# Attention folded into a mixture-of-experts layer: the first two batches by halves of their tokens, first products begun on 256 columns, and a new order of all steps

## The chip, the cores and the metric

The kernel runs on one core of a Trainium2 chip. The metric is the device time of one execution in microseconds, the median of several runs. The bulk of the work is float32 matrix products on TensorE, each built from three products of high and low parts.

## The reference

```python
def _attn_ref(x, state):                  # x: 8 x 8 x 512 x 64, state: 8 x 8 x 32 x 64
    scale = 1.0 / np.sqrt(D)
    scores = scale * np.matmul(x, state.transpose(0, 1, 3, 2))
    a = softmax(scores)                   # exp(s - max), divided by its sum + 1e-9
    xread = np.matmul(a, state)
    scores2 = scale * np.matmul(state, x.transpose(0, 1, 3, 2))
    a2 = softmax(scores2)
    sread = np.matmul(a2, x)
    return np.concatenate([xread, sread], axis=2)

def _moe_ref(x, w_in, w_out):             # tokens x 512, 512 x 2048, 2048 x 512
    h = np.maximum(x @ w_in, 0.0)
    return h * h @ w_out
```

(The two softmaxes stand in one line each here.) The 8 x 544 rows of the attention's result, with the 8 heads side by side as 512 features, go through the second function; the output is 4352 x 512 float32. The two weights come as float64.

## The kernel before, in words

`tile_attn_moe` treats each batch of 512 tokens as a block (0 to 7) and the 8 x 32 state rows as block 8. It never forms xread: the state of a batch is folded into w_in (`direct_w2`, `second_w2` and later forms make w2 = state times w_in, for 256 of the 2048 columns at a time), and the softmax of a batch, transposed and split into k_hi and k_lo, is multiplied with it. `hidden` (step hidden.BLK.FC) makes one 128-row slice of the 2048 hidden rows for the 512 tokens: six matmuls of 128x512 into a tile ph, then Relu and Square on ACT (or a VectorE form), a cast to g_hi, and on DVE the rest g_lo = ph - g_hi (for some slices PE subtracts instead, with neg_ident). `accumulate` multiplies g_hi and g_lo with wo, w_out decoded and split: eight matmuls of g_hi and four of g_lo for the four acc tiles.

Ahead of this lies the preparation. `load` brings x as tiles xn, `prep` transposes them on PE (px) and copies the result to xT (`evac`, on ACT, or on DVE where the key stands in `SECOND`). `scores` multiplies xT with the states sD into st, `keep_s` copies st to e, `transposed_scores` transposes e (pst), `softmax` takes the maximum m, subtracts (sp), exponentiates on ACT, sums (s), multiplies with the reciprocal (`sm_mul`, on POOL or DVE), transposes back (pa) and writes k_hi on ACT and k_lo on DVE. `exp_s` is the softmax the other way, over the tokens, from the same e. `load_raw`, `decode_wi` and `load_wo`, `prep_wo` bring w_in and w_out as pairs of 32-bit words and decode them: a clamp on DVE or POOL, Prelu on ACT, a shift and a SCALAR_TENSOR_TENSOR on DVE; `decode_wi` also writes the decoded part to memory (win_f), and `prep_wo` splits it with a cast on ACT and a subtraction on DVE or POOL. `warm` issues transposes of ident that nobody reads (pw).

All of this is written as generators with keys, and one table, `PLAN`, lists the keys: each time a key comes up its step goes on to its next `yield`. Everything is held in program order on every engine, so PLAN is the order of the instructions of PE, DVE, ACT, POOL and of the DMA queue of SP; a second table, `SECOND`, chooses sides. The semaphores follow from the data and the buffers. PSUM is given out by three pools: four banks for acc (the first batch's st, px, pst and pa too), two for ph (`ps_h`), two for the rest. Steps have needs (`after`), which only check that PLAN lists them late enough:

```python
            "prep": [key("load", b, 1) if g else key("start", b)],
            "keep_s": [row[key("scores", b)]],
            "exp_s": [key("transposed_scores", b, g)],
...
        ph = ps_h.tile([P, S], F32, tag="ph", name=f"ph{blk}_{fc}")
...
            mm3(ph, pairs)
```

Since all instructions go through one helper, they carry one line in the profile, L429 (L421 in the changed kernel); the names of the tiles tell them apart.

Of the kernel before, what the change touches and what calls it, by code (L numbers as in the profile page):

```python
# [11 lines left out]
F32 = mybir.dt.float32  # L12
# [46 lines left out]
    hidden.1.2 direct_w2.2 direct_w2.2 decode_wi.10 prep_wo.5 hidden.1.1 hidden.1.2 load_wo.7 accumulate.1.0
        hidden.1.1 accumulate.1.1 load_raw.7 decode_wi.6 hidden.1.2  # L60
    hidden.0.4 exp_s.0.0 hidden.1.2 decode_wi.10 decode_wi.7 decode_wi.7 prep_wo.6 hidden.1.2 second_w2.2
        hidden.1.2 prep_wo.4 decode_wi.7 hidden.0.4 prep_wo.5 exp_s.0.0 second_w2.2 load_raw.11 second_w2.2
        second_w2.2 decode_wi.7 transposes.0 load_states.2 decode_wi.7 accumulate.1.1 second_w2.2 prep_wo.8
        decode_wi.11 hidden.0.4 hidden.0.4 hidden.0.4 prep_wo.4 second_w2.2 prep_wo.6
    hidden.1.3 hidden.0.4 decode_wi.11 hidden.1.3 accumulate.1.2 prep_wo.8 load_raw.8 decode_wi.11
        hidden.1.3 hidden.1.3 transposes.0 direct_w2.3 decode_wi.11 decode_wi.8
    hidden.0.5 direct_w2.3 accumulate.1.2 hidden.0.5 decode_wi.8 direct_w2.3 direct_w2.3 hidden.0.5
        hidden.1.3 hidden.1.3 load_raw.9 direct_w2.3 decode_wi.8 hidden.0.5 prep_wo.7 accumulate.1.3
        accumulate.1.3 prep_wo.7 load_wo.13 load_wo.12 direct_w2.3 direct_w2.3 decode_wi.8 second_w2.3
        prep_wo.6 second_w2.3 hidden.0.5 decode_wi.8 accumulate.1.3 transposes.0 accumulate.1.3 decode_wi.9  # L70
        hidden.0.5 accumulate.1.3
    hidden.0.6 second_w2.3 prep_wo.9 accumulate.1.3 hidden.0.6 decode_wi.11 prep_wo.8 load_raw.12
        accumulate.0.4 load_wo.10 decode_wi.9 prep_wo.8 decode_wi.9 second_w2.3 second_w2.3
    hidden.0.7 prep_wo.7 decode_wi.9 hidden.0.6 hidden.0.6 hidden.0.7 hidden.0.7 decode_wi.9 prep_wo.7
        accumulate.0.4 hidden.0.6 hidden.0.7 prep_wo.9 prep_wo.7 prep_wo.8 second_w2.3 hidden.0.7
        accumulate.0.5 hidden.0.6 transposes.0 hidden.0.7 prep_wo.9 load_raw.14 direct.4+direct.5 prep_wo.7
        prep_wo.10 direct_w2.4 direct_w2.5 prep_wo.8 direct_w2.5 direct_w2.4 accumulate.0.5 decode_wi.12
        prep_wo.9 direct_w2.5 direct_w2.4 decode_wi.12
    hidden.1.5
    hidden.1.4 prep_wo.10 states.2 hidden.1.5 prep_wo.12 hidden.1.4 hidden.1.4 accumulate.0.6 direct_w2.4  # L80
        decode_wi.12 hidden.1.4 transposes.0 prep_wo.9 decode_wi.12 decode_wi.14 prep_wo.10 hidden.1.4
        hidden.1.5 prep_wo.10 direct_w2.5 hidden.1.4 accumulate.0.6 load_raw.13 accumulate.0.7 hidden.1.5
        hidden.1.5 decode_wi.14 hidden.1.5 prep_wo.12 exp_s.1.1 prep_wo.9 accumulate.0.7 load_w2.0.4
# [1306 lines left out]
```

## Time and profile before

| | before |
|---|---|
| median of 3 runs | 649.44 us (648.93 to 649.57) |
| profiled execution | 649.0 us, span 647.2 us |
| PE (matmuls) busy | 634.5 us, 98% |
| DVE, ACT, POOL busy | 56%, 54%, 19% |
| chain that ended last | PE 95%, DVE 3%, DMA 1% |
| granted TensorE clock, mean | 0.999 |

One execution was profiled: 647.2 us is its span, 649.0 its time with what lies around it. Busy times are those of instructions; a share of the whole span says little about a stretch with another limit, so the head (up to about 25 us, where the stream of products begins) is read from its own windows and timelines.

### The profile page before, as it was taken

How to read it: one execution, taken by the hardware profiler on the slowest of the kernel's cores; microseconds unless marked ns; L12 is line 12 of the kernel's file. 1: busy time of each engine (PE TensorE's matmuls, PEld its weight loads, DVE VectorE, ACT ScalarE, POOL GpSimd, SP SyncE). 2: the span in 40 equal slices, each digit the busy share in tenths (PEclk: the TensorE clock that was granted, in tenths of full speed). 3: DMA queues.
4: the chain of work that ended last, by engine and by line, in shares of the span. 5: the costliest groups of instructions: out<-in, count | busy, mean ns of one | idle time of the engine just before them, and what ended most of it. 6: DMA issues, size and time to landing. Idle time of an engine off the chain costs nothing.

```text
span 647.2 us, 10790 instructions
## 1 busy us (share of the span) xinstructions
PE 634.5 (98%) x4004; PEld 511.6 (79%) x4004; DVE 365.7 (56%) x658; ACT 348.0 (54%) x678; POOL 125.9 (19%) x96
## 2 busy tenths in 40 slices
PE   5899999999999999999999999999999999999997
PEld 4677777888788878778878878788777888888886
DVE  3999896775756467475347545456354554442322
ACT  3888867656655455365444544455444355444433
POOL 1584343413310220022001310021010101001000
PEclk9999999999999999999999999999999999999999
DMA  8877898988866684463665635352779814240103
GB/s 270 314 233 243 291 283 290 265 266 252 228 179 182 196 253 110 99 169 100 147 163 146 149 82 158 86 124 73 239 239 271 216 46 115 67 145 34 32 1 97
DMA packets 151859, 110.87 MB, mean 171 GB/s; under 512 B 93056, under 2 KB 126080, under 8 KB 151808
## 3 DMA queue, kind: packets, MB, share of 16 engines
q1 hardware_dynamic: 151568, 109.93, 58.7%
q8 instruction: 31, 0.51, 0.3%
q10 hardware_dynamic: 240, 0.26, 0.1%
q14 instruction: 20, 0.16, 0.1%
HBM read 71.89 MB, written 38.27 MB: 170 GB/s over the span
## 4 chain that ended last, share of the span: by engine, by line
PE 95%; DVE 3%; DMA 1%; issue 0%; SPq 0%; ACT 0%; DVEq 0%
PE acc L429 58%; PE ph L429 30%; PE w2ps L429 2%; PE w4ps L429 2%; PE pr L429 1%; PE st L429 1%; DMA xn<-in_x_dram 1%; DVE wf L429 1%; DVE s L429 1%; DVE sp L429 1%; DVE m L429 0%; PE px L429 0%; DVE dec L429 0%; SPq L429 0%; PE pw L429 0%
## 5 line engine op out<-in xcount | busy, mean ns | idle before, releaser
L429 PE MATMUL acc<-wo,g_hi 128*128 128x512 f32 x1090 | 322.4, 391 | 0.0
L429 PEld LDWEIGHTS acc<-wo,g_hi 128*128 128x128 f32 x1090 | 202.8, 188 | 47.4 <-issue 3.4
L429 PE MATMUL acc<-wo,g_lo 128*128 128x512 f32 x545 | 196.7, 389 | 0.0
L429 PE MATMUL ph<-k_hi,w 128*128 128x512 f32 x512 | 172.8, 390 | 0.2 <-DVE w L429 0.2
L429 DVE TENSOR_TENSOR g_lo<-ph,g_hi 128x512 fp32r<-128x512 f32 (+1 forms) x143 | 92.9, 655 | 83.4 <-ACT g_hi L429 81.2
L429 PEld LDWEIGHTS acc<-wo,g_lo 128*128 128x128 f32 x545 | 102.1, 188 | 21.9 <-issue 0.4
L429 ACT ACTIVATE ph<-ph 128x512 f32<-128x512 f32 (+1 forms) x150 | 83.1, 554 | 59.3 <-PE ph L429 49.7
L429 PEld LDWEIGHTS ph<-k_hi,w 128*128 128x128 f32 x512 | 96.0, 188 | 21.4 <-DVE w L429 0.6
L429 PE MATMUL ph<-k_lo,w 128*128 128x512 f32 x256 | 99.8, 390 | 0.0
L429 DVE SCALAR_TENSOR_TENSOR ph<-ph,r 128x512 f32<-128x512 f32 (+1 forms) x69 | 46.7, 676 | 87.8 <-ACT r L429 87.8
L429 ACT ACTIVATE r<-ph 128x512 f32<-128x512 f32 (+1 forms) x69 | 40.3, 583 | 86.6 <-PE ph L429 75.0
L429 POOL TENSOR_TENSOR w<-w_f,w 128x512 fp32r<-128x512 f32 x25 | 32.7, 1309 | 178.5 <-ACT w L429 167.4
L429 PEld LDWEIGHTS ph<-k_lo,w 128*128 128x128 f32 x256 | 48.0, 188 | 10.2 <-DVE k_lo L429 0.3
L429 ACT ACTIVATE g_hi<-r 128x512 fp32r<-128x512 f32 (+1 forms) x69 | 42.4, 616 | 23.1 <-PE acc L429 17.4
L429 ACT CAST g_hi<-ph 128x512 fp32r<-128x512 f32 (+1 forms) x75 | 41.7, 556 | 16.2 <-PE acc L429 14.6
L429 ACT CAST w<-w_f 128x512 fp32r<-128x512 f32 x40 | 24.6, 618 | 17.9 <-DMA w_f<-w_d 14.1
L429 POOL TENSOR_SCALAR dec<-wo_raw 128x512 f32<-128x512 f32 x10 | 20.1, 2012 | 15.3 <-DMA wo_raw<-in_moe_w_out_dram 14.9
L429 POOL TENSOR_TENSOR wo<-dec,wo 128x512 fp32r<-128x512 f32 x12 | 16.7, 1393 | 26.7 <-ACT wo L429 20.4
L429 POOL TENSOR_TENSOR sp<-sp,m 128x512 f32<-128x512 f32 x9 | 9.5, 1052 | 63.8 <-DVE m L429 63.8
L429 POOL TENSOR_TENSOR wf<-wf,wf_hi 128x512 fp32r<-128x512 f32 x8 | 10.5, 1318 | 51.8 <-ACT wf_hi L429 51.7
L429 DVE TENSOR_TENSOR ph<-ph,cross 128x256 f32<-128x256 f32 x16 | 6.9, 432 | 23.7 <-ACT cross L429 23.6
L429 POOL TENSOR_TENSOR s<-sf,s 128x512 fp32r<-128x512 f32 x6 | 7.7, 1292 | 64.8 <-ACT s L429 38.1
(115 smaller groups left out, 597.4 us busy)
## 6 DMA issues: line engine op xcount, KB each, us to landing
w_f<-w_d SPq DMA_DIRECT2D x40, 256.0 KB, 3.4
wi_raw<-in_moe_w_in_dram SPq DMA_DIRECT2D x16, 512.0 KB, 4.8
wo_raw<-in_moe_w_out_dram SPq DMA_DIRECT2D x16, 512.0 KB, 5.9
xr<-in_x_dram SPq DMA_DIRECT2D x16, 512.0 KB, 4.8
wf<-win_f SPq DMA_DIRECT2D x16, 512.0 KB, 4.3
w_d<-w4o SPq DMA_DIRECT2D x32, 256.0 KB, 3.0
w<-w2a_d SPq DMA_DIRECT2D x16, 512.0 KB, 4.5
out_dram<-o SPq DMA_DIRECT2D x31, 256.0 KB, 2.9
```

What stands on the lines that cost most here:

```text
L429: op = call(*args, **kw)
```

## The change

- The tiles xn of the first two batches hold all heads of half of the tokens each, in place of half of the heads and all tokens; `start` loads the first half, `load.B.1` the second.
- Scores of batch 0 are made by halves of the tokens (scores.0.0, scores.0.1), those of both batches with matmuls of 128 columns in place of 256. `keep_s`, `transposed_scores` and `softmax` of batches 0 and 1 go by halves of the tokens too; `keep_s` of batch 0 makes two copies for each half, on the sides that SECOND names.
- Two steps begin.0 and begin.1 (`begin`, `half_hidden`) make the first 256 columns of the products hidden.0.0 and hidden.0.1; `hidden` then does the other half of a tile that was begun.
- PLAN is written anew as a whole, and SECOND with it.

PLAN's place around the first products:

```diff
-        warm.3 load_wo.4 decode_wi.3 prep_wo.0 softmax.0.0 prep_wo.1 decode_wi.3 scores.1 keep_s.1.0
-        keep_s.1.1 softmax.0.1 decode_wi.3
-    hidden.0.0 decode_wi.3 hidden.0.0 hidden.0.0 transposed_scores.1.0 hidden.0.0 load_raw.5 load_wo.6
+        prep_wo.2 prep_wo.0 decode_wi.3 scores.1 softmax.0.1 decode_wi.3 prep_wo.2 begin.1 prep_wo.0
+        softmax.0.1 decode_wi.3 keep_s.1.1
+    hidden.0.1 keep_s.1.0 transposed_scores.1.0 prep_wo.0 transposed_scores.1.1
+    hidden.0.0 decode_wi.3 load_wo.1 decode_wi.3 exp_s.0.0 prep_wo.2 hidden.0.1 softmax.1.1 hidden.0.1
+        softmax.1.0 load_raw.5 begin.0 decode_wi.4 softmax.1.1 hidden.0.1 softmax.1.0 hidden.0.0 hidden.0.0
...
```

SECOND (DVE in place of ACT for keep_s and xT, POOL in place of DVE for the clamps, DVE in place of POOL for sm_mul and w_out_lo), and the code:

```diff
-    decode_wi: 2 4 5 6 14 15
-    decode_wo: 0 3 4 5 6 9 10 12 13 15
+    decode_wi: 4 5 6 8 9
+    decode_wo: 0 3 4 5 6 7 8 9 12 13 14 15
+    keep_s: 0.0.0 0.1.1
-    sm_mul: 0.0 3.0 4.0 4.1 6.1
+    sm_mul: 3.0 6.0 7.1
-    w_out_lo: 3 9 13 15
+    w_out_lo: 0 3 8 11
-    xT: 0.0.0 0.0.1 0.1.1
...
-                xn = p2.tile([P, 4, KC, D], F32, tag="xp", name=f"xn{b}_{g}", bufs=NXP)
+                xn = p2.tile([P, 2 * NC, 2 * D], F32, tag="xp", name=f"xn{b}_{g}", bufs=NXP)
...
-                    nc.sync.dma_start(xn[:, h].rearrange("p h k d -> p h (k d)"), self.rows(g)[:, h])
+                    nc.sync.dma_start(xn[:, ts(c, NC)], self.rows(c)[..., ts(g, 2 * D)])
...
+        def half_scores(self, a):
+            b, calls = self.b, []
...
-                                nc.tensor.matmul, self.st[m][32 * c : 32 * c + 32, o], state_t(b, m, g, c),
-                                self.x[c // 2][64 * m : 64 * m + 64, c % 2, o],
+                                nc.tensor.matmul, self.st[m][32 * c : 32 * c + 32, ts(2 * a + g, P)],
+                                state_t(b, m, g, c), self.x[a][64 * m : 64 * m + 64, c // 2, ts(2 * (c % 2) + g, P)],
...
-        def keep_s(self, g):
+        def keep_s(self, i):
...
+            for m in range(2):
+                if m:
+                    yield
+                evac(f"keep_s.{b}.{i}.{m}", pair[:, i, :, m], st[m][:, i])
...
+    ph_begun = {}
+
+    def half_hidden(fc, ph, a):
+
+        whi, wlo = weights[0, fc // 2]
+        cs, t = ts(fc % 2, P), ts(a, HB)
+        khi, klo = att[0].k
+        pairs = [((whi[:, c, cs], wlo[:, c, cs]), (khi[:, c, t], klo[:, c, t])) for c in range(G)]
+        mm3(ph[:, t], pairs, first=a == 0, skip=True)
+
+    def begin(fc):
+
+        ph_begun[fc] = ps_h.tile([P, S], F32, tag="ph", name=f"ph0_{fc}")
+        half_hidden(fc, ph_begun[fc], 0)
+
     def hidden(blk, fc, nt):
...
-        ph = ps_h.tile([P, S], F32, tag="ph", name=f"ph{blk}_{fc}")
-        if blk == B:
+        ph = None
+        if blk or fc not in ph_begun:
+            ph = ps_h.tile([P, S], F32, tag="ph", name=f"ph{blk}_{fc}")
+        if ph is None:
+            ph = ph_begun.pop(fc)
+            half_hidden(fc, ph, 1)
+        elif blk == B:
...
+    for fc in range(2):
+        step(key("begin", fc), begin, fc, after=[key("softmax", 0, 0), key("direct_w2", 0)])
```

The first place in the order is PE at the first products of block 0 (ph0_0 and ph0_1 are the products 0.0 and 0.1, pst1 transposes of batch 1's e, acc0_0 the first accumulators). In before, from the last part of product 0.0 on:

```order
L429 MATMUL ph0_0_418<-k_hi0_125,w2_0_0_259 128x512
L429 MATMUL pst1_0_430<-ident_73,e21_413 128x128 [waits Activation_49] x2
L429 MATMUL pst1_0_430<-ident_73,e21_413 128x128 x2
L429 MATMUL pst1_1_447<-ident_73,e21_413 128x128 x4
L429 MATMUL ph0_1_459<-k_hi0_125,w2_0_0_259 128x512
L429 MATMUL ph0_1_459<-k_lo0_126,w2_0_0_259 128x512
L429 MATMUL ph0_1_459<-k_hi0_125,w2_0_0_259 128x512 x2
L429 MATMUL ph0_1_459<-k_lo0_126,w2_0_0_259 128x512
L429 MATMUL ph0_1_459<-k_hi0_125,w2_0_0_259 128x512
L429 MATMUL acc0_0_0_471<-wo0_390,g_hi0_0_426 128x512 [waits Activation_49]
```

and in the change, from the last of pst1 on (product 0.1 stands ahead of these rows, in twelve matmuls of 128x256):

```order
L421 MATMUL pst1_1_462<-ident_73,e21_447 128x128 x3
L421 MATMUL ph0_0_467<-k_hi0_125,w2_0_0_267 128x512
L421 MATMUL ph0_0_467<-k_lo0_126,w2_0_0_267 128x512
L421 MATMUL ph0_0_467<-k_hi0_125,w2_0_0_267 128x512 x2
L421 MATMUL ph0_0_467<-k_lo0_126,w2_0_0_267 128x512
L421 MATMUL ph0_0_467<-k_hi0_125,w2_0_0_267 128x512
L421 MATMUL ph0_0_496<-k_hi0_125,w2_0_0_267 128x256 [waits DVE_49]
L421 MATMUL ph0_0_496<-k_lo0_126,w2_0_0_267 128x256
L421 MATMUL ph0_0_496<-k_hi0_125,w2_0_0_267 128x256 x2
L421 MATMUL ph0_0_496<-k_lo0_126,w2_0_0_267 128x256
L421 MATMUL ph0_0_496<-k_hi0_125,w2_0_0_267 128x256
L421 MATMUL ph0_1_436<-g_hi0_1_484,neg_ident_138 128x512 [waits Activation_49]
```

The two products have changed places; product 0.0 is whole, and six matmuls of 256 columns into a second tile ph0_0 follow it, the first with a wait on a DVE semaphore, with neg_ident (for ph0_1) behind them; acc0_0 of g_hi0_0, which followed the products, now comes after neg_ident and w2ps.

The second place is DVE ahead of g_lo0_0 (dec is a part of w_out in decoding, wf of w_in, m11 and sp1 the softmax of batch 1, m20 and nb20 of exp_s.0.0). In before:

```order
L429 TENSOR_SCALAR dec2_440<-wo_raw2_316 128x512 [waits DMAHW4_49]
L429 TENSOR_REDUCE m11_0_444<-pst1_0_430 128x16 [waits PE_49]
L429 TENSOR_REDUCE m11_1_453<-pst1_1_447 128x16 [waits PE_49]
L429 TENSOR_TENSOR sp1_1_452<-pst1_1_447,m11_1_453 128x512 [waits DVE_49,Pool_49]
L429 TENSOR_TENSOR sp1_0_443<-pst1_0_430,m11_0_444 128x512
L429 TENSOR_TENSOR g_lo0_0_427<-ph0_0_418,g_hi0_0_426 128x512 [waits Activation_49]
```

and in the change:

```order
L421 TENSOR_REDUCE m20_0_478<-e20_216 128x1
L421 TENSOR_SCALAR nb20_0_480<-m20_0_478 128x1 [waits DVE_49]
L421 TENSOR_REDUCE m11_1_488<-pst1_1_462 128x16 [waits PE_49]
L421 TENSOR_REDUCE m11_0_492<-pst1_0_456 128x16
L421 TENSOR_TENSOR sp1_1_487<-pst1_1_462,m11_1_488 128x512 [waits DVE_49,Pool_49]
L421 TENSOR_TENSOR sp1_0_491<-pst1_0_456,m11_0_492 128x512 [waits DVE_49,Pool_49]
L421 TENSOR_SCALAR wf2_379<-wf2_379 128x512 [waits DMAHW0_49,Activation_49]
L421 TENSOR_SCALAR dec1_513<-wo_raw1_475 128x512 [waits DMAHW6_49]
L421 SCALAR_TENSOR_TENSOR wf2_379<-wi_raw4_363,wf2_379 128x512 [waits DMAHW3_49,DVE_49]
L421 TENSOR_TENSOR g_lo0_0_508<-ph0_0_467,g_hi0_0_507 128x512 [waits Activation_49]
```

g_lo0_0 was the 38th instruction of DVE and is the 42nd; the reduction and nb of exp_s.0.0 and a part of wf2 now stand just ahead of it.

The third place is the DMA queue of SP at its start (xn0_0 and xn0_1 are the x of batch 0, two DMAs each). In before:

```order
L429 DMA xn0_0_127<-in_x_dram 128x2x256 x2
L429 DMA wi_raw0_130<-in_moe_w_in_dram 128x2x512
L429 DMA std0_134<-in_state_dram 128x2x64
L429 DMA xn0_1_136<-in_x_dram 128x2x256
L429 DMA wi_raw1_145<-in_moe_w_in_dram 128x2x512
L429 DMA xn0_1_136<-in_x_dram 128x2x256
L429 DMA std0_134<-in_state_dram 128x2x64
L429 DMA std0_134<-in_state_dram 128x2x64 [waits DMAHW0_49]
L429 DMA wo_raw1_169<-in_moe_w_out_dram 128x1024 [waits DMAHW1_49]
L429 DMA win_f0_77<-wf0_132 128x512 [waits DMAHW2_49,DVE_49]
```

and in the change:

```order
L421 DMA xn0_0_127<-in_x_dram 128x4x128 x2
L421 DMA wi_raw0_133<-in_moe_w_in_dram 128x2x512
L421 DMA std0_149<-in_state_dram 128x2x64 x3
L421 DMA wi_raw1_161<-in_moe_w_in_dram 128x2x512
L421 DMA xn0_1_172<-in_x_dram 128x4x128
L421 DMA win_f0_77<-wf0_140 128x512 [waits DMAHW0_49,DVE_49]
L421 DMA xn0_1_172<-in_x_dram 128x4x128 [waits DMAHW1_49]
L421 DMA wi_raw2_205<-in_moe_w_in_dram 128x2x512 [waits DMAHW2_49]
```

The second DMA of xn0_1 stood ahead of win_f0, and now stands behind it; win_f0 waits on a DVE semaphore.

## Rows read from the trace of the kernel before

**Rows 1.** The page, part 1: busy us (share of the span) xinstructions of each engine.

```profile
PE 634.5 (98%) x4004; PEld 511.6 (79%) x4004; DVE 365.7 (56%) x658; ACT 348.0 (54%) x678; POOL 125.9 (19%) x96
```

**Rows 2.** Waits of PE over the whole span: us in total, times, longest.

```profile
PE ph L429 <- DVE w L429: 0.2, 1, 0.2
```

**Rows 3.** Windows: busy us of PE, PEld, DVE, ACT, POOL (instructions), PEclk, DMA share, GB/s.

```profile
8.10:11.20 3.10, 3.05 (x15) 3.02 (x16) 2.78 (x6) 1.61 (x4) 0.00 (x0) 1.00 1.01 349
20.00:31.30 11.30, 10.01 (x91) 7.51 (x98) 11.09 (x21) 9.83 (x20) 6.10 (x5) 1.00 0.83 287
```

**Rows 4.** Timeline of PE, 24 to 36 us: start us, us, engine, instruction, count [idle before].

```profile
24.27 1.09 PE L429 MATMUL st<-xT,sD 64*32 64x256 f32 x32
25.30 0.51 PE L429 MATMUL ph<-k_hi,w 128*128 128x512 f32 x1
...
29.14 2.02 PE L429 MATMUL acc<-wo,g_hi 128*128 128x512 f32 x8
...
32.45 1.09 PE L429 MATMUL acc<-wo,g_lo 128*128 128x512 f32 x4
...
34.85 0.73 PE L429 MATMUL ph<-k_hi,w 128*128 128x512 f32 x2 [0.18 <-DVE w L429]
```

**Rows 5.** Timeline of DVE from 18 to 33 us.

```profile
21.54 1.28 DVE L429 TENSOR_SCALAR wf<-wf 128x512 uint32<-128x512 uint32 x1
...
30.56 0.68 DVE L429 TENSOR_TENSOR g_lo<-ph,g_hi 128x512 fp32r<-128x512 f32 x1
```

**Rows 6.** Timeline of ACT from 25 to 33 us.

```profile
25.70 1.06 ACT L429 COPY e<-st 128x512 f32<-128x512 f32 x2
27.08 1.20 ACT L429 ACTIVATE ph<-ph 128x512 f32<-128x512 f32 x2 [0.32 <-PE ph L429]
28.31 0.59 ACT L429 CAST g_hi<-ph 128x512 fp32r<-128x512 f32 x1
```

**Rows 7.** Groups of DVE, 7 to 31.3 us: busy us, mean ns of one | idle before.

```profile
L429 DVE TENSOR_SCALAR wf<-wf 128x512 uint32<-128x512 uint32 x4 | 3.0, 761 | 0.8 <-ACT wf L429 0.7
...
L429 DVE TENSOR_REDUCE m<-pst 128x16 f32<-128x512 f32 x4 | 2.7, 685 | 1.1 <-PE pst L429 1.1
L429 DVE COPY xT<-px 128x512 f32<-128x512 f32 x3 | 2.1, 686 | 0.5 <-PE px L429 0.5
...
L429 DVE TENSOR_SCALAR wf<-wi_raw 128x512 f32<-128x512 f32 x3 | 1.3, 426 | 7.2 <-DMA wi_raw<-in_moe_w_in_dram 7.2
...
L429 DVE TENSOR_TENSOR sp<-sp,s 128x512 f32<-128x512 f32 x1 | 0.7, 677 | 0.0
```

**Rows 8.** Groups of DVE, 14 to 60 us.

```profile
L429 DVE TENSOR_TENSOR w<-w2ps,w 128x256 fp32r<-128x256 f32 x7 | 2.9, 408 | 0.1
```

**Rows 9.** Timeline of POOL from 17 to 32 us.

```profile
21.26 1.27 POOL L429 TENSOR_TENSOR wo<-dec,wo 128x512 fp32r<-128x512 f32 x1
```

**Rows 10.** Timeline of PE from 636 to 641 us (six rows of 128x256 from first to last).

```profile
637.07 0.40 PE L429 MATMUL acc<-wo,g_hi 128*128 128x256 f32 x2
...
637.79 0.63 PE L429 MATMUL acc<-wo,g_hi 128*128 128x512 f32 x2
```

**Rows 11.** Timeline of SP (its DMA issues) from 0 to 26 us.

```profile
3.78 0.47 SPq L429 DMA_DIRECT2D xn<-in_x_dram  x1
...
9.98 0.34 SPq L429 DMA_DIRECT2D win_f<-wf  x1
...
13.94 0.74 SPq L429 DMA_DIRECT2D xn<-in_x_dram  x1
```

**Rows 12.** DMA issues, 0 to 40 us: KB each, median us to landing.

```profile
xn<-in_x_dram SPq DMA_DIRECT2D x8, 256.0 KB, 5.9
```

**Rows 13.** Timeline of PE from 7 to 13 us.

```profile
8.15 1.97 PE L429 MATMUL px<-ident,xn 128*128 128x128 f32 x8 [2.09 <-DMA xn<-in_x_dram]
...
11.19 0.68 PE L429 MATMUL px<-ident,xn 128*128 128x128 f32 x4
```

**Rows 14.** Tile pw: duration ns min/median/max, first and last start us.

```profile
L429 PE MATMUL pw<-ident x24: 270/372/421, 4.6 to 24.1; 128*128 128x128 f32 x24
```

More of the change, by code (lines that the diff above doesn't have):

```diff
@@ L59 @@
[L59 to L83, printed above, removed]
-        accumulate.0.7 accumulate.0.7 prep_wo.10 prep_wo.12
-    hidden.1.6 load_w2.0.4 accumulate.0.7 prep_wo.10 decode_wi.12 accumulate.0.7
@@ new lines @@
+    hidden.4.11 last_w2.2 transposes.4 load_w2.5.0 hidden.4.10 hidden.4.11 hidden.4.10 hidden.4.11
+        hidden.4.11 start.7 softmax.5.1 hidden.4.11 exp_s.5.1 hidden.4.11 softmax.5.0
+    hidden.4.12 accumulate.2.15 load_w2.4.7 hidden.4.12 accumulate.4.9
+    hidden.4.13 softmax.5.0 hidden.4.13 accumulate.4.10 hidden.4.12 hidden.4.13 softmax.5.0 load_w2.5.0
+        hidden.4.12 load_w2.5.1 exp_s.5.0 softmax.5.1 softmax.5.1 hidden.4.12 hidden.4.13 hidden.4.12
+        accumulate.4.11 transposes.4
@@ new lines @@
+    hidden.6.6 softmax.7.0
+    hidden.6.8 accumulate.6.4 hidden.6.8 hidden.6.8 hidden.6.6 last_w2.6 hidden.6.6 accumulate.6.5
+        softmax.7.0 hidden.6.8 hidden.6.8 hidden.6.6 hidden.6.8 hidden.6.6 softmax.7.1
+    hidden.6.7 last_w2.6 hidden.6.7 load_wi.0 hidden.6.7 hidden.6.6 w2.7+read.6 hidden.6.7 accumulate.6.6
+        softmax.7.0 exp_s.7.0 transposes.7 load_wi.0 sread.6 hidden.6.7 last_w2.7 hidden.6.7 last_w2.7
+        transposes.7
+    hidden.6.9 sread.6 sread.6 hidden.6.9 hidden.6.9 hidden.6.9
@@ L363 @@
 """
 ROWS = """
-    scores.0
     scores.1
@@ L646, in prep @@
                 pt = pool.tile([P, S], F32, tag=tag, name=f"px{b}_{g}_{c}")
[L647 to L650 removed]
+                for i in range(NC):
+                    nc.tensor.transpose(pt[:, ts(i, P)], self.xn[g][:, NC * c + i], ident)
                 yield
@@ L1267, in needed, with scores_0 @@
         }[kind]
+    def scores_0(a):
+        if a == 0:
+            att[0].st = {m: ps_acc.tile([P, S], F32, tag="acc", name=f"st0_{m}") for m in range(2)}
+        in_a_row(att[0].half_scores(a))
     row = {}
+    for a in range(2):
+        step(key("scores", 0, a), scores_0, a, after=[key("prep", 0, a), [key("states", 0), key("scores", 0, 0)][a]])
+    row["scores.0"] = key("scores", 0, 1)
     for members in [line.split() for line in ROWS.strip().split("\n")]:
@@ L1296, in tile_attn_moe @@
                 del after["keep_s"]
+            else:
+                after["exp_s"] = [key("transposed_scores", b, i) for i in range(G)]
+            if b == 0:
+                after["keep_s"] = [key("scores", 0, g)]
+                after["transposed_scores"] = [key("keep_s", 0, g)]
             for name, needs in after.items():
```

666 lines of the change are left out of this document (333 added, 333 removed), and 3 rows, old and new, of the table SECOND.

## The prediction

> **What bounds the kernel.** I read the page first: TensorE (PE) is busy for 634.5 us, 98% of the span, VectorE (DVE) for 365.7, 56% [rows 1]. The waits of PE come next: the only wait of a product for an operand is one of 0.2 us [rows 2]. So PE is the bound. Time can be won in the head, before the stream of products begins at 25.30 us, or lost where something new stops that stream. The windows then tell who sets the pace of the head: from 20.0 to 31.3 us DVE works 11.09 of 11.30 us [rows 3]. While PE enters its stream, DVE has no slack at all; the whole argument rests on this. The timeline of PE gives the places: scores of batch 1 at 24.27, first product at 25.30, the first acc at 29.14, with the transposes pst and the second product between these two [rows 4].
>
> **What the new order does.** The diff means to begin the first two products early, on 256 columns. In the order of PE that is not what stands there. begin.1 comes after scores.1 and the last pa, and is followed at once by the other half of the same product: twelve matmuls of 256 columns where six of 512 stood. And hidden.0.0 stands ahead of begin.0, so product 0.0 runs whole, and begin.0 then fills a second tile ph0_0 with six matmuls of 256 columns that nobody reads. That tile takes the PSUM bank of the first one, so its first matmul waits on DVE for the bank's last reader, the subtraction g_lo0_0. PE works in order: behind that wait stand neg_ident, the 32 w2ps of block 1, all of acc 0.0 and product 0.2, and none of these needs g_lo0_0 or its bank, but for the last four of acc. In before PE waited for nothing there: behind the product stood pst, the second product and acc, and g_lo0_0 was wanted only at 32.45, by the last four matmuls of acc [rows 4].
>
> **The wait, step by step.** In before g_lo0_0 ran from 30.56 to 31.24 [rows 5], while its product was done when Relu began, at 27.08 [rows 6]: 4.2 us. Its own chain is shorter: Relu and Square 1.20, cast 0.59 [rows 6], subtraction 0.68 [rows 5], some 2.5 us. The other 1.7 us is the queue of DVE. So DVE's queue sets the time at which the new wait ends, and I count that queue. In before 37 instructions stand ahead of g_lo0_0 on DVE, now 41. Gone are three copies of xT (3 x 0.686) and one multiply of sp (0.677) [rows 7], 2.74 us; they go to ACT and POOL. New are one clamp of wf (0.43), one shift (0.43 where nothing blocks it, like the clamp), one SCALAR_TENSOR_TENSOR and one reduction m<-e (like the other reduction, 0.69 each), one subtraction for wo (like the multiply, 0.68) [rows 7], nb (128x1, at most a clamp; I take 0.2), and two copies of half an e, 256 columns each (like the 128x256 w, 0.41 [rows 8]): 3.9 us. That is net +1.1 us in a stretch without slack. I add 0.3, because the multiply that left DVE now runs on POOL, and a shift of wf beside a POOL instruction took 1.28 us, 0.85 more than a clamp [rows 5, 7, 9]. So g_lo0_0 ends at about 31.24 + 1.4 = 32.65.
>
> [...]
>
> PE does the same useful work up to there: product, pst and second product took from 25.30 to 29.14, 3.84 us [rows 4]. The pieces of 256 columns cost little: six start within 0.72 us (637.07 to 637.79 [rows 10]), twelve 1.44, where the six of 512 were part of the 3.84 with about 1.4. With the start unchanged PE reaches begin.0 at 29.2 and stands until 32.65: a **wait of about 3.4 us** in one piece. Then come the six unread matmuls, 0.72 us.
>
> **The start.** This is the term I know least, and it cancels: as long as DVE sets the end of the wait, an earlier start only makes the wait longer. The first half of x (two DMAs ahead of all) can go on alone, but the second DMA of the other half now stands on SP behind win_f, which waits for the first decoded w_in: it was issued at 3.78 us, win_f at 9.98 [rows 11], and an x takes 5.9 us more to land [rows 12]. The copies of xT are all on ACT now, and both pa and the scores of batch 1 stand ahead of the first product on PE. Bounds: not before batch 1's x is there (13.94 + 5.9 = 19.8 [rows 11, 12]), transposed (four in 0.68 [rows 13]), copied (like e, 0.53 [rows 6]) and scored (1.09 [rows 4]), 22.1; not much after the 1.4 us that DVE is later, 26.9 with a little queueing. I take 25.3, the old start, since DVE is as full before it as it was.
>
> **The sum.** What began at 29.14 in before (acc and w2ps) begins when g_lo0_0 is done and the unread matmuls are through: 32.65 + 0.72 - 29.14 = +4.2 us. PE's wait of 0.18 at 34.85 was for w of DVE [rows 4]; behind the long wait DVE has caught up, so I take off 0.2. The rest of the program keeps its matmuls, and before's PE waited for nothing in it [rows 2]. The new sides of decode, squares and stores there I cost at nothing, because PE's stream covers them: DVE is busy for 56% of the span [rows 1], so a us put on it there moves nothing; without that cover each would cost its own 0.4 to 0.7 us. Sum +4.0: the profiled execution, 649.0, becomes 653.0. The median of the runs, 649.44, lies 0.4 above that execution, and I forecast **653.3**.
>
> Bounds of that sum: at the low end DVE uses up all it stood idle in this stretch (1.1 + 0.5 + 0.7 [rows 7]) and the 0.85 of the long shift, g_lo0_0 ends at 31.24 + 1.1 - 3.15 = 29.2, and the total is +0.6, 649.6 to 650.0; its own chain behind the earliest start would end at 22.1 + 3.9 + 2.5 = 28.5, so DVE decides there too. At the high end it ends 2 us later (two more long shifts, or a late wo_raw, whose clamp stands just ahead of it): 655.3.
>
> **The rivals.** About 0.2%, 1.3 us, is what a measurement of this kernel can tell from no change.
>
> Slower pace after the wait (0.20). In the trace eight transposes at 8.15 us took 1.97 us, and four at 11.19 only 0.68 [rows 13]. [...] If a wait of 3.4 us brings that back, 3.0 us at half pace cost 1.5 us: 654.8. For it: the wait is longer than the 2.09 us of idle time ahead of 8.15. Against it: the trace has no stop in mid-stream that shows it.
> [...]
>
> DVE later by 1.5 us (0.08): 654.8 as well, by blocked shifts or by the DMA of wo_raw.
>
> DVE early (0.10): with the copies gone DVE runs ahead, g_lo0_0 ends at 29.2 to 29.6, PE waits for it hardly at all: 649.6 to 650.4, no change that can be told.
>
> Faster (0.08): begin.0 doesn't do what its place in the order says, its product is dropped or finds its bank free, and PE does not stop. Then each us by which the first product starts before 25.3 is won, at most 3.2 (22.1); half of that gives 647.8. It decides at a start of about 24.0. For it: the first half of x needs only the two DMAs ahead of all. Against it: 24 unread transposes pw run in the trace of before [rows 14], and the wait stands in the order.
>
> **The numbers.** Forecast 0.54 (652 to 654.5), pace 0.20, DVE later 0.08, DVE early 0.10, faster 0.08. The range leaves out "faster", most of "DVE early" and a little above: 650.2 to 656.2. Faster by over 0.2%: 0.08; within: 0.09, nearly all of "DVE early"; slower: 0.83.
>
> **What would show it.** In the waits of PE one entry of 3 to 4 us of ph for DVE's g_lo; in the groups, eighteen matmuls 128x256 of ph<-k at the head; in the timeline g_lo0_0 ending at 32 to 33 and the first product at 25; behind the wait matmuls at twice their old spacing if the pace falls, at the old one if not. I am wrong if that entry is missing or under 1 us, or if PE waits for more than 1 us in all after 40 us.

## The result, and the profile after

The changed kernel takes 656.34 us (median of 4 runs, 655.82 to 657.57), the kernel before 649.51 (648.93 to 650.01) beside it: a ratio of 1.0104 [1.0090, 1.0117], 6.8 us slower. The forecast was 653.3 with a range from 650.2 to 656.2. The profiled execution took 657.57 us, 1.2 above its median, so local times below are larger than what the medians tell.

The page of the changed kernel, part 1 and the group of the products' matmuls in part 5:

```profile
PE 641.4 (98%) x4080; PEld 515.4 (79%) x4080; DVE 358.7 (55%) x659; ACT 345.6 (53%) x675; POOL 132.0 (20%) x100
...
L421 PE MATMUL ph<-k_hi,w 128*128 128x512 f32 (+1 forms) x520 | 175.9, 390 | 3.6 <-DVE g_lo L421 3.2
```

PE is busy 6.9 us longer than in [rows 1], with DVE 7.0 us less: DVE's total says nothing of the loss. The group's idle time has a new releaser, g_lo. Waits of PE in the changed kernel (us in total, times, longest):

```profile
PE ph L421 <- DVE g_lo L421: 3.2, 1, 3.2
...
PE pr L421 <- DMA xr<-in_x_dram: 0.5, 1, 0.5
PE ph L421 <- DVE w L421: 0.3, 1, 0.3
```

One entry of 3.2 us stands where [rows 2] had 0.2; the other two lie behind 40 us. Its place, in the timeline of PE (start us, us, engine, instruction, count [idle before]), from the scores of batch 1 on:

```profile
24.94 1.45 PE L421 MATMUL st<-xT,sD 64*32 64x128 f32 x64
26.32 0.39 PE L421 MATMUL ph<-k_hi,w 128*128 128x256 f32 x1
...
27.85 1.04 PE L421 MATMUL pst<-ident,e 128*128 128x128 f32 x8
...
29.88 0.40 PE L421 MATMUL ph<-k_hi,w 128*128 128x512 f32 x1
33.49 0.58 PE L421 MATMUL ph<-k_hi,w 128*128 128x256 f32 x1 [3.21 <-DVE g_lo L421]
...
34.93 0.63 PE L421 MATMUL ph<-g_hi,neg_ident 128*128 128x512 f32 x1
35.49 1.96 PE L421 MATMUL w2ps<-wf,sD 64*32 64x256 f32 x32
37.38 2.98 PE L421 MATMUL acc<-wo,g_hi 128*128 128x512 f32 x8
40.20 0.39 PE L421 MATMUL ph<-k_hi,w 128*128 128x512 f32 x1
...
651.57 0.39 PE L421 MATMUL acc<-wo,g_lo 128*128 128x512 f32 x1
```

The first product starts at 26.32 (25.30 in [rows 4]). PE stands before the unread product, and everything behind it is slow: the six matmuls take 1.44 us (33.49 to 34.93) where six took 0.72 [rows 10], eight acc 2.98 where [rows 4] have 2.02. The windows of the same kernel (busy us of PE, PEld, DVE, ACT and POOL, then PEclk, DMA share, GB/s) say why:

```profile
28.00:32.00 4.00, 2.28 (x15) 1.67 (x12) 3.97 (x9) 3.90 (x8) 3.44 (x3) 1.00 0.58 187
32.00:33.00 1.00, 0.00 (x0) 0.00 (x0) 1.00 (x3) 0.76 (x2) 0.00 (x0) 0.72 0.43 164
33.00:35.00 2.00, 1.51 (x7) 1.51 (x7) 1.09 (x2) 0.00 (x0) 1.83 (x1) 0.50 0.64 198
35.00:39.00 4.00, 4.00 (x38) 2.05 (x38) 1.04 (x3) 1.44 (x4) 0.12 (x1) 0.50 0.95 341
39.00:40.00 1.00, 1.00 (x6) 0.77 (x5) 0.97 (x2) 1.00 (x3) 0.00 (x0) 0.86 0.99 406
40.00:42.00 2.00, 2.00 (x10) 1.65 (x9) 1.89 (x6) 0.75 (x3) 1.67 (x2) 1.00 0.25 102
```

The granted clock falls from 1.00 to 0.50 while PE stands, and comes back only in the slice from 39 to 40. Last, DVE and ACT around g_lo0_0:

```profile
32.15 0.68 DVE L421 SCALAR_TENSOR_TENSOR wf<-wi_raw,wf 128x512 uint32<-128x512 uint32 x1
32.75 0.68 DVE L421 TENSOR_TENSOR g_lo<-ph,g_hi 128x512 fp32r<-128x512 f32 x1
```
```profile
30.31 1.20 ACT L421 ACTIVATE ph<-ph 128x512 f32<-128x512 f32 x2
31.54 0.59 ACT L421 CAST g_hi<-ph 128x512 fp32r<-128x512 f32 x1
```

g_hi is there at 32.13, g_lo0_0 runs from 32.75 to 33.43.

The last matmul of the program started at 643.03 in the profile of before and starts at 651.57 now. These 8.5 us are accounted for by:

| place | us | from |
|---|---|---|
| later first product | +1.0 | 26.32 - 25.30 |
| PE stands for g_lo0_0 | +3.4 | 33.49 - (29.88 + 0.23) |
| unread product at the full clock | +0.7 | six starts, [rows 10] |
| half clock from the unread product to acc | +2.7 | (40.20 - 33.49) - 0.72 - (32.45 - 29.14 of [rows 4]) |
| small gaps of before up to 35 us that are gone | -0.4 | the remainder up to 42 us |
| behind 42 us | +1.1 | small gaps; 0.5 and 0.3 of them stand in the waits above |

### The profile page after: what moved, and what is told of

Read it like the earlier page. It is cut to its first block, busy times and chain, and to the rows that moved or that the text cites. A ratio compares the mean times of both kernels' runs of the same rounds, so it can differ in the third digit from the quotient of the medians.

```text
span 655.8 us, 10979 instructions
## 1 busy us (share of the span) xinstructions
PE 641.4 (98%) x4080; PEld 515.4 (79%) x4080; DVE 358.7 (55%) x659; ACT 345.6 (53%) x675; POOL 132.0 (20%) x100
## 4 chain that ended last, share of the span: by engine, by line
PE 87%; DMA 5%; DVE 3%; ACT 2%; issue 1%; SPq 1%; POOL 0%; DVEq 0%; ACTq 0%
PE acc L421 52%; PE ph L421 28%; PE w2ps L421 3%; DMA wi_raw<-in_moe_w_in_dram 2%; PE w4ps L421 2%; PE pr L421 1%; DMA xp<-in_x_dram 1%; PE st L421 1%; DVE wf L421 1%; SPq L421 1%; DMA xr<-in_x_dram 1%; DMA e_d<-turned 1%; DMA w_d<-w2o 0%; ACT xT L421 0%; DVE w4o L421 0%
## 5 line engine op out<-in xcount | busy, mean ns | idle before, releaser
L421 PE MATMUL ph<-k_hi,w 128*128 128x512 f32 (+1 forms) x520 | 175.9, 390 | 3.6 <-DVE g_lo L421 3.2
L421 ACT ACTIVATE ph<-ph 128x512 f32<-128x512 f32 (+1 forms) x164 | 92.3, 565 | 82.2 <-PE ph L421 78.2
L421 PE MATMUL ph<-k_lo,w 128*128 128x512 f32 (+1 forms) x260 | 101.0, 388 | 0.0
L421 DVE SCALAR_TENSOR_TENSOR ph<-ph,r 128x512 f32<-128x512 f32 (+1 forms) x62 | 41.1, 662 | 78.4 <-ACT r L421 78.3
L421 ACT ACTIVATE r<-ph 128x512 f32<-128x512 f32 (+1 forms) x62 | 35.2, 571 | 86.2 <-PE ph L421 79.9
L421 ACT CAST g_hi<-ph 128x512 fp32r<-128x512 f32 (+1 forms) x82 | 46.5, 567 | 18.0 <-PE acc L421 16.2
L421 ACT ACTIVATE g_hi<-r 128x512 fp32r<-128x512 f32 (+1 forms) x62 | 37.4, 604 | 18.7 <-PE acc L421 13.3
L421 POOL TENSOR_TENSOR s<-sf,s 128x512 fp32r<-128x512 f32 x9 | 11.9, 1326 | 111.4 <-ACT s L421 71.4
L421 POOL TENSOR_TENSOR sp<-sp,s 128x512 f32<-128x512 f32 x13 | 14.0, 1078 | 40.4 <-DVE s L421 26.1
L421 DVE COPY w4o<-w4ps 128x512 f32<-128x512 f32 x21 | 13.8, 683 | 11.7 <-PE w4ps L421 8.8
```

What stands on the lines that cost most here:

```text
L421: op = call(*args, **kw)
```

## The experiments

Three theories stood against each other: that the stop for g_lo0_0 alone costs what is lost (the forecast); that the pace behind the stop costs as much again (the rival with 0.20); and that the rest of the new order loses time even without the stop. Ratios are to the kernel before on the same chip, whose medians lay between 649.30 and 649.77.

### The stop taken away in two ways: e1_begin_first and e2_no_begin0

```diff
-    hidden.0.0 decode_wi.3 load_wo.1 ...
-        softmax.1.0 load_raw.5 begin.0 decode_wi.4 ...
+    begin.0 hidden.0.0 decode_wi.3 load_wo.1 ...
+        softmax.1.0 load_raw.5 decode_wi.4 ...
```

> The changed kernel with begin.0 ahead of hidden.0.0, so that its six matmuls are the first half of product 0.0 and nothing is computed in vain. Theory A (the misplaced begin.0 costs its wait of 3.4 us, its 0.7 us of unread matmuls and about 2.9 us of matmuls at the lower clock behind the wait): 656.3 - 7.0 = 649.4, no wait of ph for g_lo, granted clock 1.00 from 30 to 40 us. Rival B (the wait only shows that DVE is late; without it PE waits for the same DVE a little later, at the first acc and at product 0.2): short waits of 1.5 to 2.5 us in sum, clock 1.00, about 651.5.

```diff
-        softmax.1.0 load_raw.5 begin.0 decode_wi.4 ...
+        softmax.1.0 load_raw.5 decode_wi.4 ...
-    for fc in range(2):
+    for fc in range(1, 2):
```

> The changed kernel without begin.0 at all: product 0.0 in six matmuls of 512 columns. Theory A: 649.3; rival B: 651.4. Against the run with begin.0 ahead of the product it tells what the cut into 256 columns costs for this product: 0.06 us by its spacing, nothing that can be measured; if the cut itself were worth anything, this run would be slower by over 0.5.

Measured: 652.60 [1.0031, 1.0061] and 652.62 [1.0030, 1.0058]. In both the stop is gone and the clock reads 1.00 from 25 to 45 us. Half of the loss goes with begin.0's place: 3.7 us in the medians. The other half stays: 3.1 us, with no wait of PE over 0.9 us behind the first product in either. What stays shows in the trace of e2_again, the same kernel run once more (below): its only wait of PE between 26 and 46 us, and the weight loads (PEld) at 31 us:

```profile
PE pa L421 <- DVE w L421: 0.7, 1, 0.7
```
```profile
31.19 0.19 PEld L421 LDWEIGHTS ph<-g_hi,neg_ident 128*128 128x128 f32 x1 [0.53 <-ACT g_hi L421]
...
32.28 0.61 PEld L421 LDWEIGHTS w2ps<-wf,sD 64*32 64x32 f32 x30 [0.40 <-DVE sp L421]
```

and in its windows (columns as above):

```profile
30.00:35.00 5.00, 4.82 (x45) 2.79 (x44) 5.00 (x11) 4.94 (x11) 3.81 (x3) 1.00 0.58 188
35.00:40.00 5.00, 5.00 (x23) 4.12 (x23) 4.86 (x10) 4.58 (x11) 3.21 (x4) 1.00 0.98 326
40.00:45.00 5.00, 4.28 (x23) 3.46 (x23) 4.96 (x10) 3.83 (x10) 5.00 (x4) 1.00 0.40 157
```

The same 15 us in the kernel before:

```profile
30.00:45.00 15.00, 14.78 (x94) 10.96 (x94) 14.01 (x28) 12.12 (x26) 12.89 (x9) 1.00 0.77 276
```

DVE works 14.8 of 15 us in e2_again, but 14.0 in before too, where PE hardly waits; so a full DVE alone does not explain it. In e2_again PE waits for DVE at 42 us, and at 31 us loads weights late, behind ACT and DVE: neg_ident and w2ps take from 30.93 (last product at 30.70, 0.23 each) to acc at 33.30, 2.4 us, where the same two take 0.32 + 1.02 behind the fill of e6 (next section). Together that is 1.7 us. The profiled executions split what stays. In six without a stop (e1, e2's two, and e5, e9 and e10 below; e12 has a longer wait of its own) the first product starts 0.9 to 2.2 us later than in [rows 4] (26.17 in e9, 27.45 in e2), and from it to the last matmul it takes 1.5 to 2.9 us longer (619.2 in e2, 620.6 in e1, against 643.03 - 25.30 = 617.7).

The start differs as much between executions. Seven of the profiled executions have the new order unchanged up to the first product (the changed kernel, e1, e2, e2_again, e3, e11, e12); it starts between 25.50 (e11) and 27.79 (e3). In before and two variants with its head (e4, e8) it starts between 25.08 and 25.39. The three latest of the seven are e2's two and e3, and in these the clock of the head read lower, as in this window of e2_again, where the changed kernel, e1 (from 21 us on) and e12 read 1.00 and e11 has four px in 0.60 us at 22.12 (1.06 at 23.08 in e2):

```profile
20.00:25.00 5.00, 4.21 (x25) 4.15 (x26) 3.83 (x9) 4.28 (x10) 2.07 (x2) 0.66 1.07 386
```

### The stop filled, so that the clock holds: e3_fill, e6_fill_head and e7_after_head

```diff
     def begin(fc):
...
+        if fc == 0:
+            fill = ps_acc.tile([P, S], F32, tag="acc", name="fill")
+            for _ in range(14):
+                nc.tensor.matmul(fill, weights[0, 0][0][:, 0, :P], att[0].k[0][:, 0], start=True, stop=True)
```

> The changed kernel with 14 unread matmuls of 128x512 into a free bank between product 0.0 and begin.0, some 3.2 us of work at 0.227 us each, so that TensorE works where it stood; the wait for g_lo0_0 ends when it did. If the clock falls because TensorE stands still: granted clock 1.00 from 30 to 40 us, and the 2.9 us are back, 656.3 - 2.9 = 653.4. If the fall of the clock had another cause, or the slow matmuls behind the wait were slow for lack of operands: 656.3 as before, with the clock at 0.5 in the same place.

Measured 655.86 [1.0080, 1.0115], a miss: only 0.5 us less than the changed kernel. The clock did hold (1.00 from 28 to 42 us), and from pst to the product ph_2 it took 9.60 us instead of 12.35. But in this execution's head the clock read 0.50 between 11 and 14 us and 0.66 between 20 and 25, and the first product came at 27.79. So the head was given 24 more unread transposes, with the fill and without it:

```diff
-    WARM = 12
+    WARM = 24
-        ... load.0.1 states.0 scores.0.0
+        ... load.0.1 states.0 warm.12 warm.13 warm.14 warm.15 warm.16 scores.0.0
-        ... second_w2.0 warm.2 prep.1.0
+        ... second_w2.0 warm.2 warm.17 warm.18 warm.19 warm.20 warm.21 warm.22 warm.23 prep.1.0
```

> The changed kernel with the head filled in the same way and, besides, the 14 unread matmuls in the wait for g_lo0_0. If the half clock behind the wait is worth what the first profile shows (2.75 us from pst to product 0.2: 12.35 against 9.60), this run is faster than the one with the filled head alone by 2.5 to 3: about 652.8. If a fall of the clock costs nothing in the end: the same as that one.

> The changed kernel with the head filled, and the wait for g_lo0_0 left empty: the control for the run before it. 656.3 less what a falling clock in the head costs in some executions, 655.5; mean clock 0.995, from the wait alone.

e6 took 653.65 [1.0037, 1.0081], e7 655.60 [1.0071, 1.0114]: 1.95 us, though the intervals overlap. The timelines of PE show the mechanism where it acts. With the fill, then with PE left standing:

```profile
33.17 0.38 PE L423 MATMUL ph<-k_hi,w 128*128 128x256 f32 x1
...
34.31 1.09 PE L423 MATMUL w2ps<-wf,sD 64*32 64x256 f32 x32
35.33 2.12 PE L423 MATMUL acc<-wo,g_hi 128*128 128x512 f32 x8
37.29 0.40 PE L423 MATMUL ph<-k_hi,w 128*128 128x512 f32 x1
```
```profile
33.03 0.39 PE L423 MATMUL ph<-k_hi,w 128*128 128x256 f32 x1 [3.06 <-DVE g_lo L423]
...
34.17 1.71 PE L423 MATMUL w2ps<-wf,sD 64*32 64x256 f32 x32
35.81 3.08 PE L423 MATMUL acc<-wo,g_hi 128*128 128x512 f32 x8
38.73 0.39 PE L423 MATMUL ph<-k_hi,w 128*128 128x512 f32 x1
```

The same instructions take 4.12 us with the fill and 5.70 without, 1.6 more; in the changed kernel 6.71, 2.6 more. The granted clock of e7 in the stretch behind its stop:

```profile
33.00:35.00 2.00, 1.97 (x31) 1.50 (x39) 0.39 (x1) 0.00 (x0) 1.42 (x1) 0.88 0.93 234
35.00:38.00 3.00, 3.00 (x23) 1.80 (x6) 1.66 (x4) 2.06 (x6) 0.00 (x0) 0.51 0.97 343
```

In e6 it reads 1.00 in both. So the pace behind the stop is the clock, and costs 1.6 to 2.7 us on PE's path. That this comes out at the end of the kernel is borne by the two medians alone: e6's profiled execution takes 655.72, e7's 654.63, and from first product to last matmul 623.6 against 622.6, since in e6's PE waits again at 88 and 92 us, 0.3 us for wo of POOL and 1.6 us for g_lo.

The falls behind g_lo0_0's wait came behind idle time of PE, 3.21 us in the changed kernel and 3.06 in e7, and none came where the fill took its place (1.00 in e3 and e6); but in e7 it came after PE had resumed (last section).

With its stop filled, begin.0 costs nothing that the medians show: e6 and the kernel without begin.0 and with the same head (e5, next) both take 653.65. Their intervals reach 1.3 to 1.4 us to either side, and in the profiled executions the way from first product to last matmul is 3.2 us longer in e6 (623.6 against 620.4); so this equality is not firm.

### The head: e5_no_begin0_head, e9_x_ahead, e10_x_ahead_dve

e5 is e2 with the head's 24 transposes as above.

> The changed kernel without begin.0, and with 24 unread transposes more in the head: 10 ahead of the first scores (where TensorE stood for sD) and 14 ahead of batch 1's first px (where it stood for x), some 1.1 and 1.5 us of work. Theory: the new head leaves TensorE so little to do at 8 to 10 and 19 to 21 us that the clock falls in some executions; with the holes filled it reads 1.00 in all, and the median falls from 652.62 to 651.5 (the two executions without begin.0 whose mean clock was 1.000 took 651.47 and 651.71). Rival: the clock of the head costs nothing that counts, since DVE sets the start of the products: 652.6, or more by what the transposes delay.

Measured 653.65 [1.0039, 1.0078], with the clock at 1.000 in four of five executions. The median did not fall, but the filling has a price of its own: in the chain that ended last, 18 unread transposes, 14 of them the new ones, stand ahead of batch 1's px (start us, us, what), and the first product comes at 27.25 (at 26.15 and 26.01 in e6 and e7, whose head is the same):

```profile
19.71 2.20 PE pw L423 x18
```

So e5 does not tell the head's clock from its own transposes; e9 does. It is e2 with the second half of x issued ahead of win_f:

```diff
-        prep.0.0 load.0.1 prep.0.0 states.0 warm.11 decode_wi.0 decode_wi.1 load.0.1 states.0 scores.0.0
+        prep.0.0 load.0.1 load.0.1 prep.0.0 states.0 warm.11 decode_wi.0 decode_wi.1 states.0 scores.0.0
```

> The changed kernel without begin.0, and with the second DMA of batch 0's other half of x ahead of win_f on SP, as in the kernel before (issued at about 4.9 in place of 10.4 us). If this DMA is what makes the head late (the products of the four profiles of the new head start 1 to 2.5 us behind before's 25.30): px of that half at 11 to 12 us in place of 13, and the products up to 1.5 us earlier, 651.2. If DVE or ACT sets the start anyway: px earlier, the products not, 652.6 as without begin.0.

and e10 gives DVE its three copies of xT back on top of that:

```diff
+    xT: 0.0.0 0.0.1 0.1.1
```

> The same with three of batch 0's copies of xT back on DVE, 2.1 us of it, as in the kernel before. If ACT is what is late in the new head: 0.5 to 1 us earlier than the run before it. If DVE is: up to 2 us later.

Measured 652.65 [1.0029, 1.0059] and 652.62 [1.0033, 1.0060], with first products at 26.17 and 26.29. Neither the order of x nor the side of xT holds the 3.1 us. Nor does the head's clock: the four executions of e9 with a mean clock of 1.000 took 651.50 to 653.01, 2.2 to 3.7 us more than before. It may hold a part, since e2's two executions at 1.000 took 651.47 and 651.71 and its other three 652.62 to 653.59.

### A stop in the kernel before: e4_before_dead

```diff
+    def dead(n):
...
+        ph = ps_h.tile([P, S], F32, tag="ph", name="dead")
...
+        mm3(ph[:, :HB], pairs, skip=True)
-    hidden.0.1 softmax.1.0 hidden.0.1 ...
+    hidden.0.1 dead.0 softmax.1.0 hidden.0.1 ...
```

> The kernel before with the misplaced product alone: six unread matmuls of 256 columns into a new ph tile behind the second product. They wait for g_lo0_0, which ends at 31.24, from 29.14 on: 2.1 us of wait and 0.7 us of matmuls. If the clock holds through a wait of 2.1 us: 649.5 + 2.8 = 652.3, less a few tenths. If it falls here too, for as long as in the changed kernel: 655.

Measured 652.44 [1.0029, 1.0059], a hit. Timeline of PE and a window of this kernel:

```profile
31.38 0.39 PE L429 MATMUL dead<-k_hi,w 128*128 128x256 f32 x1 [1.98 <-DVE g_lo L429]
...
32.20 2.00 PE L429 MATMUL acc<-wo,g_hi 128*128 128x512 f32 x8
```
```profile
30.00:35.00 5.00, 3.62 (x46) 2.63 (x46) 3.04 (x7) 1.72 (x4) 4.51 (x4) 1.00 1.02 383
```

An unread product that waits for g_lo0_0 costs wait and matmuls, 1.98 + 0.82, and here the clock reads 1.00 behind it: eight acc take their 2.00 us. The price of such a stop is its length plus, in some stops (1.6 us behind 3.06 in e7), the clock.

### The product's own chain, or DVE's queue: e11_glo_early

```diff
-        hidden.0.0 hidden.0.0 decode_wi.4 prep_wo.1 decode_wi.4 prep_wo.1 ...
-        load_raw.6 hidden.0.0 accumulate.0.0 ...
+        hidden.0.0 hidden.0.0 hidden.0.0 decode_wi.4 prep_wo.1 decode_wi.4 prep_wo.1 ...
+        load_raw.6 accumulate.0.0 ...
```

> The changed kernel, begin.0 and all, with g_lo0_0 three instructions earlier on DVE (ahead of the two of wf2 and the clamp of dec1, 1.5 us). If DVE's queue sets the end of the wait, as the prediction had it: the wait 1.5 us shorter, 654.8 or less. If the product's own chain does (in the changed kernel's trace g_hi0_0 is cast until 32.13, and g_lo0_0 began at 32.75): 0.6 us shorter, 655.7.

Measured 655.60 [1.0074, 1.0111], a hit for the chain. With three instructions fewer ahead of it, g_lo0_0 stands idle for ACT's g_hi (timeline of DVE):

```profile
31.34 0.69 DVE L421 TENSOR_TENSOR g_lo<-ph,g_hi 128x512 fp32r<-128x512 f32 x1 [0.47 <-ACT g_hi L421]
```

PE still waits 2.6 us. DVE's queue held the end of the wait for 0.6 us only (32.13 to 32.75 in the changed kernel); the rest is Relu, Square and cast on ACT and the subtraction. The clock falls behind this shorter stop too (window as above, PE resumed at 32.09):

```profile
33.00:35.00 2.00, 2.00 (x35) 0.87 (x33) 1.10 (x2) 0.37 (x1) 1.56 (x1) 0.50 0.21 73
```

### The later order alone: e8_late_order

The order and sides of before up to its hidden.0.4, the new order and sides from its hidden.0.4 on:

```diff
-    hidden.0.4 exp_s.0.0 hidden.1.2 decode_wi.10 decode_wi.7 decode_wi.7 prep_wo.6 ...
+    exp_s.0.0 second_w2.2 exp_s.0.0 second_w2.2 ...
+    hidden.0.4 accumulate.1.1 decode_wi.8 transposes.0 ...
```

> The kernel before up to product 0.4 (about 62 us) in code, order and sides, and from there the changed kernel's order and sides. The changed kernel's profile shows four waits of TensorE behind 60 us that before's has not (at 78, 93, 144 and 526 us), 1.3 us in all. If they belong to the late order itself: 650.8. If they come from the late head: 649.5, as before.

Measured 655.68 [1.0073, 1.0112]: a miss, since the seam between the two orders makes a stop of its own. Timeline of PE and the window behind it:

```profile
58.23 1.10 PE L89 MATMUL w2ps<-wf,sD 64*32 64x256 f32 x32 [2.78 <-DVE wf L89]
...
59.93 1.05 PE L89 MATMUL ph<-k_hi,w 128*128 128x512 f32 x2
60.78 0.63 PE L89 MATMUL ph<-k_lo,w 128*128 128x512 f32 x1
```
```profile
58.50:63.00 4.50, 4.50 (x42) 3.23 (x27) 2.88 (x6) 2.30 (x6) 2.68 (x2) 0.64 0.47 138
```

The clock falls here too, behind 2.78 us. Of the 5.4 us by which the stretch from first product to last matmul grew (623.11 against 617.73), 2.8 is the stop and some 1.5 the clock (3.3 us of matmuls 0.43 apart instead of 0.23); about 1 us would be left for the later order. With the seam's own work in it, that stays a bound.

### DVE relieved: e12_less_dve and the control e2_again

e2 with wo0's subtraction back on POOL, and the reduction and nb of exp_s.0.0 behind the product 0.2: some 1.5 us less on DVE up to there.

```diff
-    hidden.0.0 decode_wi.3 load_wo.1 decode_wi.3 exp_s.0.0 prep_wo.2 ...
+    hidden.0.0 decode_wi.3 load_wo.1 decode_wi.3 prep_wo.2 ...
-        hidden.0.2 decode_wi.5 exp_s.0.1
+        hidden.0.2 decode_wi.5 exp_s.0.0 exp_s.0.1
-    w_out_lo: 0 3 8 11
+    w_out_lo: 3 8 11
```

> The changed kernel without begin.0, and with two of DVE's new pieces put elsewhere: wo0's subtraction back on POOL, and the reduction and nb of exp_s.0.0 behind product 0.2 in the order; 1.5 us less of DVE ahead of g_lo0_0. Without begin.0 DVE is busy for 14.2 of 15 us from 30 to 45 us while TensorE stands for 0.2 and 0.8 us. If DVE's queue is what is left of the loss of 3.1 us: 651.2 to 651.5. If it is the head ahead of 25 us, or POOL (5.00 of 5 us at 40 to 45) takes DVE's place: 652.6 or later.

> The control on the same chip: the changed kernel without begin.0 once more, 652.6.

Measured 655.39 [1.0066, 1.0093] against 653.05 [1.0032, 1.0059] for the control: this way of taking work from DVE made it 2.3 us slower. DVE and POOL in e12:

```profile
32.31 1.50 DVE L421 TENSOR_SCALAR dec<-wo_raw 128x512 f32<-128x512 f32 x1
33.73 1.14 DVE L421 SCALAR_TENSOR_TENSOR wf<-wi_raw,wf 128x512 uint32<-128x512 uint32 x1
34.79 0.68 DVE L421 TENSOR_TENSOR g_lo<-ph,g_hi 128x512 fp32r<-128x512 f32 x1
...
42.04 0.67 DVE L421 TENSOR_REDUCE m<-e 128x1 f32<-128x512 f32 x1
...
43.60 0.41 DVE L421 TENSOR_TENSOR w<-w2ps,w 128x256 fp32r<-128x256 f32 x1
```
```profile
32.08 1.45 POOL L421 TENSOR_TENSOR wo<-dec,wo 128x512 fp32r<-128x512 f32 x1
33.49 2.14 POOL L421 TENSOR_SCALAR wf<-wi_raw 128x512 f32<-128x512 f32 x1
```

The clamp takes 1.50 us beside POOL's subtraction (0.42 in the changed kernel), the SCALAR_TENSOR_TENSOR 1.14 (0.68 above), and g_lo ends at 35.47 (34.10 in the control). PE's wait for w behind it grows from 0.7 to 1.9 us. This w comes 2.1 us later than in the control (43.60 against 41.50): 1.4 us of it is there when g_lo ends, and the rest is about what the moved reduction and its nb take (0.8 us from 42.04 on), which now stand ahead of this w with those of exp_s.0.1. So e12 took work away from one wait and put part of it ahead of the next, and does not tell what a relieved DVE would be worth.

The clamp ends at 33.81, 0.3 us behind POOL's subtraction (33.53). The SCALAR_TENSOR_TENSOR ends at 34.87, while POOL's instruction beside it runs to 35.63. What held the two up is not shown.

## Why the prediction was right in kind and too low in size

The step that failed is the sum behind the stop: it left out the pace, and put the start ("it cancels") and the rest of the program ("I cost at nothing") at nothing. Along PE's path in the profiled execution the runs show in its place a half clock that cost 2.7 us, a start 1.0 us later and 1.1 us of gaps behind 42 us. By taking begin.0 away they show that 3.7 us go with it and 3.1 us stay. The two accounts differ because the stop covers waits that come to light once it is gone.

- **The mechanism held, the wait's length in part by luck.** begin.0's product is made whole and read by nobody, its first matmul waits for g_lo0_0, and the wait stands as one entry: 3.2 us idle, 3.4 with the last product's 0.2, as forecast. But both of its ends came later than forecast by about the same: PE reached begin.0 at 30.1, not 29.2, and g_lo0_0 ended at 33.43, not 32.65. The groups show twelve k_hi and six k_lo matmuls 128x256, the eighteen foreseen. Faster or unchanged did not come.
- **The pace was mis-sized, and given too little chance.** "Against it: the trace has no stop in mid-stream that shows it" was true of the trace of before, and I set 0.20 on it and 1.5 us. Its 3.0 us were the way from 8.15 to 11.19 in [rows 13], its half pace my estimate, which no row of before shows; the runs showed 0.50 for some 6.8 us in the changed kernel, and 0.50 to 0.51 for some 3.3 us in e7 and e11. It came: clock 0.50, at a cost of 1.6 us (e7 against e6, local), 1.95 (their medians) or 2.7 (the profiled execution). Along PE's path it is the largest term that the sum lacks: the profiled execution lies 4.5 us above the sum, of which the pace is 2.7, the later start 1.0 and the gaps behind 42 us 1.1, less some small gaps that are gone.
- **"DVE's queue sets the time at which the new wait ends" held by 0.6 us only.** e11 takes three instructions out of that queue and gains 0.6 us of wait; then ACT sets it. The queue of before was 1.7 us longer than the product's own chain, that of the change only 0.6, because the product itself ends later: the new order puts product 0.1 and pst ahead of it, and all of it starts later. The prediction saw that order but did not carry it into the chain: with product 0.0 done at 29.14 and 2.5 us of chain behind it, g_lo0_0 could not end before about 31.6, so the 29.2 of its low bound and of "DVE early" was out of reach unless the start came earlier. (Its count of DVE, 3.9 less 2.74, is 1.2 and not 1.1. That POOL blocks a shift, on which its 0.3 and "DVE later" lean, no run shows; the five shifts of wf up to g_lo0_0 took 0.41 to 0.66 us in the changed kernel.)
- **So "it cancels" failed too.** I held that an earlier or later start of the products only changes the wait's length. Where the product's own chain sets the end, a later start moves the end with it. The start came at 26.32, not 25.3, in the profiled execution, and that 1.0 us went into its time.
- **"The rest of the program ... I cost at nothing" failed.** Without any stop 3.1 us stay (e1, e2), which the profiled executions put on a later start, 0.9 to 2.2 us, and on the stream behind it, 1.5 to 2.9. The cover I named, DVE busy for 56% of the span, is an average: from 30 to 45 us DVE is busy for 14.0 us in before and 14.8 without begin.0, and PE meets it and ACT at two places (1.0 us around w2ps, 0.7 for pa). In before no wait of PE stood behind 42 us; in the change and its variants 0 to 2 us do (the longest 1.6 us in e6), differing from one profiled execution to the next.
- **The 0.2 taken off for DVE catching up was too small.** begin.0 puts 6.8 us on PE's path in the changed kernel (3.4 + 0.7 + 2.7), and taking it out returns 3.7 in the medians: while PE stood, DVE and ACT went on (busy for 3.40 and 2.59 of 3.40 us from 30.1 to 33.5), and the 1.7 us that e2_again loses at 31 and 42 us is not lost there. The stop lay partly on work that would have been waited for anyway; the other 1.4 us is little more than the 1.2 by which the profiled execution lies above its median. So the 4.0 us that the forecast gave to begin.0 came out near the 3.7 it is worth, because the pace that it left out is about made up for by what taking the stop away does not return; that is luck. By this account the 3.1 us of the rest are the whole shortfall.

What stays open is what holds these 3.1 us: which part of the new order makes the start late, and which makes the stream behind it longer. The second half of x and the side of batch 0's xT do not, and the head's clock holds a part at most; e12 moved work from one wait to the next and does not answer it. From 20 to 25 us ACT is busy for 4.64 of 5 us in the changed kernel and for 4.11 in before, a place where no run looked for it. No version tried here beat the kernel before.

## What to carry to other kernels

Look in the order for a product that is issued twice: here a tile that took the buffer of one still being read stopped PE for 3.21 us, and with it all that stood behind in PE's order, though nobody read the tile. Price such a stop at its length plus the clock behind it (1.98 us and no fall in e4, 3.21 us and 2.7 in the changed kernel), and fill it with unread matmuls on a free buffer to see the two apart, as e6 against e7. Before moving work "to an engine that is half idle", read that engine's busy time in the stretch where it is waited for (DVE: 56% of the span, but 14.0 of 15 us from 30 to 45), and how long its instructions take beside the other engine's work (a clamp 1.50 us beside POOL's subtraction in e12, 0.42 in the changed kernel). When work is taken from ahead of one wait, look which wait it stands ahead of now.
